# Attention followed by two MLPs: five of nine probability tiles of a head pair turned by TensorE in float32, with a float32 product with V

## The chip, the core and the metric

The kernel runs on one core of a Trainium2 chip. Five engines work side by side, each with an instruction queue of its own that is worked off in order: TensorE (PE) multiplies and transposes, VectorE (DVE) and ScalarE (ACT) do elementwise work and empty PSUM, GpSimd (POOL) does elementwise work between SBUF tiles, and SyncE (SP) issues transfers. The metric is device time in microseconds; lower is better.

## What is computed

```python
q_rot, k_rot = rotate(q), rotate(k)                  # 2 batches, 8 heads, 576 positions, width 64
scores = scale * q_rot @ k_rot.T
attn = exp(scores - max) ; attn /= attn.sum + 1e-9   # P, 576 x 576 for each head
x = (attn @ v)                                       # -> 1152 tokens x 512
h = x @ w_in ;  g = h * tanh(softplus(h)) ; x2 = g @ w_out      # 512 -> 2048 -> 512
h = x2 @ w_in2; g = h * sigmoid(1.702 h)  ; out = g @ w_out2
```

All of it is in float32 accuracy. The MLP weights come as 64-bit numbers and are narrowed on the core.

## The kernel before

**Two stretches.** Attention goes first, then the two MLPs, which are long dense runs of products on PE. Attention handles heads in pairs: 8 pairs, one after the other, overlapped by the order of the code.

**One pair.** Queries and keys are rotated (`rope_ops`), turned on PE (`turn`: 8 transposes for q, 8 for k, 3 instructions for the last 64 positions) and split by ACT and DVE into a high and a low part, tile `qk`. The 576 queries of two heads make nine tiles of 128 rows: tiles 0 to 7 are four chunks c of two heads each (tile n is head n % 2 of chunk n // 2), and tile 8 holds the last 64 queries of both heads. For each tile PE makes the scores (`s_mm`, 12 matmuls for the two heads of a chunk, 6 for tile 8) into a slot of two PSUM banks, `st`; DVE finds the row maximum (`s_max`, L260); ACT takes the exponential into the float32 tile `e` or `er` (`s_exp`, L275).

**Turning P.** The product with V needs P with keys on partitions. In most tiles P is split into a high and a low half-precision part: the high part by ACT or DVE (`p_split`, L288 or L290), the low part mostly by POOL (L294), into a tile `p`; a transposing transfer (`p_turn`, L339) writes it to `pt`. In pairs 0 to 6 tiles 7 and 8, and in the last pair tiles 4 to 8, go another way: PE transposes `e` in float32 (`e_turn`: one idle matmul and 5 transposes, `et`), and ACT or DVE write the high part to `pt` and DVE the low part (`e_part`).

**Product with V.** Group 0 holds chunks 0 and 1 (256 columns), group 1 holds chunks 2 and 3 and tile 8 (320 columns). `pv_mm` runs 5 blocks of keys by 3 terms (high by high, high by low, low by high) by 2 heads: 30 half-precision matmuls into the bank `pvps`, each head on its own 64 output columns of the array. The row sums, inverted and turned on PE (`r_mm`, `rps`), scale the result (`pv_end`), which becomes `x`.

**PSUM.** Three slots of two banks (`pss`, tag "s") take the score tiles and the turned tiles `et`; one bank (`bank`, tag "m") is shared by `tps` (turned q and k), `rps` and `vps`; one bank is `pvps`. A new tenant of a slot or of the shared bank waits until its last one has been read.

**Order.** `Plan` plays all attention operations through with written-down costs and ranks (`RANK`), chooses an engine where several are allowed, and writes the code in the order of the starts. Where it sees PE idle for more than 0.2 and `pvps` is not collecting a product, it puts idle matmuls (`keep_clock`, L641, 128x192, here called fillers). The MLP begins with products `h`, and pieces of the last pair's second product stand between them.

Of the kernel before, what the change touches and what calls it, by code (L numbers as in the profile page):

```python
# [22 lines left out]
def kernel(  # L23
# [62 lines left out]
    QK, vh, PT, sums, rrs, vs = ({} for _ in range(6))  # L86
# [13 lines left out]
    raw = [att.tile([128, 2, 2, (4, 4, 5)[i], 64], F32, name=f"raw{i}", bufs=1) for i in range(3)]  # L100
    P2 = [att.tile([128, 2, 2, KB * 128], F16, name=f"p2_{i}", bufs=1) for i in range(3)]
    x = xp.tile([128, 2, KD, TOK], F32R, tag="x", name="x")

    def heads(p):
        return p // NPAIR, 2 * (p % NPAIR)

    def load(ps, i):
# [3 lines left out]
        SP.dma_start(  # L111
            out=raw[i][:, j:j + len(ps), :, 0:4, :].rearrange("p j a t d -> p (j a) (t d)"),
            in_=src.rearrange("a (p t) d -> p a (t d)", t=4),
        )
# [6 lines left out]
    def load_v_rest(ps):  # L121
        src = v.rearrange("b h s d -> (b h) s d")[2 * ps[0]:2 * ps[-1] + 2, MAIN:S, :]
        SP.dma_start(
            out=raw[2][0:64, :, :, 4, :].rearrange("p j a d -> p (j a) d"), in_=src.rearrange("a s d -> s a d")
        )

    def v_max(ps):

        t = att.tile([128, 4], F32, tag="vs", name="vs", bufs=2)
        for j, p in enumerate(ps):  # L130
            vs[p] = t
            ACT.activation(
                out=junk, in_=raw[2][:, j].rearrange("p a t d -> p (a t d)"), func=AF.Abs, scale=1.0 / VEXP,
                accum_out=t[:, 2 + j:3 + j],
            )
# [12 lines left out]
    def v_high(p, eng):  # L148
        t = vh[p] = att.tile([128, 2, 2, KB, 64], F16, tag="vh", name="vh")
        if eng is ACT:  # L150
            ACT.activation(out=t[:, 0], in_=raw[2][:, p % 2], func=AF.Copy, scale=vs[p][:, 0:1])
        else:
            eng.tensor_scalar(t[:, 0], raw[2][:, p % 2], vs[p][:, 0:1], 1.0, op0=ALU.mult, op1=ALU.mult)

    def v_low(p):
        t = vh[p]
        DVE.scalar_tensor_tensor(  # L157
            out=t[:, 1], in0=raw[2][:, p % 2], scalar=vs[p][:, 0:1], in1=t[:, 0], op0=ALU.mult, op1=ALU.subtract
        )
# [147 lines left out]
    def pt_tile(p, g):  # L307
        if (p, g) not in PT:
            PT[p, g] = att.tile([128, 4 * KB, GW[g]], F16, tag=f"pt{g}", name=f"pt{g}")
# [4 lines left out]
    def e_turn(p, n):  # L314

        ps = pss.tile([128, 2, 512], F32, tag="s", name="et").rearrange("p b c -> p (b c)")[:, 0:KB * 128]
        e = ebuf[p, n // 2][:, n % 2]
        PE.matmul(out=ps[:, S - 64:KB * 128], lhsT=idle[:, 0:128], rhs=idle[:, 0:128], start=True, stop=True)
        for kb in range(KB):
            k = min(128, S - 128 * kb)  # L320
            PE.transpose(ps[0:k, 128 * kb:128 * kb + 128], e[:, 128 * kb:128 * kb + k], ident)
        return ps.rearrange("p (k q) -> p k q", q=128)

    def e_part(p, n, ps, eng, hl):
        c, h = n // 2, n % 2
        if n < 8:
            t = pt_tile(p, c // 2)[:, :, COL[c]:COL[c] + 128]
            ts = [t[:, KB * (2 * h + i):KB * (2 * h + i) + KB] for i in range(2)]
        else:
            t = pt_tile(p, 1)[:, :, 128:192].rearrange("k (h i b) q -> k h i b q", h=2, i=2)  # L330
            ts = [t[:, :, i] for i in range(2)]
            ps = ps.rearrange("k b (h q) -> k h b q", h=2)
        p_split(eng, hl, ts, ps)
# [310 lines left out]
    class Plan:  # L644
# [5 lines left out]
            raw0=1, raw1=1, raw2=1, rest=1, diag=1, rtmp0=3, rtmp1=2, m=1, pv=1, qk=2, s=3, nm=4, e=3,  # L650
            er=1, p2=3, pt0=2, pt1=2, sums=2, rc=2, rr=1, rrr=2, rb0=2, rb1=2, xf=2, vs=2, vh=2,
# [5 lines left out]
        WINDOW, BUSY = 10.24 / 3, 3400  # L657
        PORT = {"rope", "rest", "first rope", "first rest", "high", "low", "v low", "xh", "xl", "w", "rr", "rw"}
# [44 lines left out]
        def play(self):  # L703
# [10 lines left out]
            order, moved, work = [], 0.0, {}  # L714
# [23 lines left out]
            while True:  # L738
# [17 lines left out]
                if e == "PE":  # L756
# [10 lines left out]
                    done = product(start, o["cost"][e] + 0.1 * (o["rank"][1] != last), o["work"])  # L767
                    last = o["rank"][1]
                else:
                    done = start + o["cost"][e]  # L770
                free[e] = done
                if e == "POOL":
# [26 lines left out]
            self.work = work  # L799
# [8 lines left out]
        "rw": 6664.6, "rw DVE": 7052.1, "rw POOL": 5435.6, "first": 5746.8, "load q": 6506.8, "load k": 6297.4,  # L808
        "load rest": 5690.8, "load v": 5839.4, "load w": 7656.6, "rest": 7370.3, "rope": 6798.8, "turn": 4961.8,
        "v max": 5287.7, "v high": 6725.5, "v low": 5649.6, "s": 6645.6, "max": 4994.2, "exp": 5948,  # L810
        "high": 7357.5, "low": 5556, "pt": 7298.5, "rc": 4907.1, "rr": 6797.4, "rm": 7136.3, "rb": 6944.6,
        "pv": 7853.9, "xf": 7140.7, "xh": 6655.5, "xl": 5772.8, "w": 5847.2, "u": 6863.7, "first load q": 5110.4,
        "first load k": 5319.2, "first load rest": 5774.5, "first rope": 7126.2, "first rope POOL": 5698.3,
        "first turn": 5576.8, "first rest": 7569.6, "first rest DVE": 5260.8, "rest DVE": 6867.2,
        "rope POOL": 6505.7, "high DVE": 6486.6, "low DVE": 7209.9, "xh DVE": 7381.7, "xl DVE": 5695.4,
        "et": 5024.9, "eh": 4889.8, "el": 6845.6, "v high ACT": 7107, "w POOL": 5692.1, "rr ACT": 7178.7,
        "rr DVE": 6476.3, "eh DVE": 6583.4, "load sin": 6991.7, "load cos": 7296.4,
# [4 lines left out]
    PV_CUTS = (0, 5, 10, 15)  # L822
# [3 lines left out]
    turns_of = [SOME_TURNS] * (NP - 1) + [PE_TURNS]  # L826
    ET8 = 5
    uses = []
    for p in range(NP):
        late = [("et", p - 1, n) for n in turns_of[p - 1] if n < 8] if p else []  # L830
        for n in TILES[p]:
            uses.append(("s", p, n))
            if n == 3:
                uses += late
            if n == ET8:
                uses.append(("et", p, 8))
    uses += [("et", NP - 1, n) for n in PE_TURNS if n < 8]
# [29 lines left out]
    def plan_v(ps):  # L867
# [3 lines left out]
            needs=[("raw", p, 2), ("st", p, 1)] + [("qk", 0, 2)] * (p == 0), makes=("vm", p), holds=[("raw2", p // 2)] + hold)  # L871
# [9 lines left out]
    def plan_pair(p):  # L881
# [22 lines left out]
        last = p == NP - 1  # L904
        turns = turns_of[p]

        def first(n):
            d["s", n] = s_tile()
            s_mm(p, [(n, d["s", n], 0)])

        def second(n):
            parts = [(n, d["s", n], 1)]
            if n % 4 < 3:
                d["s", n + 1] = s_tile()
                parts.append((n + 1, d["s", n + 1], 0))
            s_mm(p, parts)

# [11 lines left out]
        for at, n in enumerate(TILES[p]):  # L929
            g, c = base + at, n // 2  # L930
            s_at = ring["s", p, n]
            e, p2 = (("e", 4 * p + c), ("p2", 4 * p + c)) if n < 8 else (("er", p), None)
# [11 lines left out]
            if n in turns:  # L944
                gr = min(c // 2, 1)
                hold = [ring["et", p, n], (f"pt{gr}", p + 2 * gr)]
                add("PE", 0.6, (g, "et"), lambda n=n: d.update({("et", n): e_turn(p, n)}), work=640,
                    needs=[("en", p, n)], makes=("et", p, n), holds=hold + [e])
                add(None, dict(ACT=0.684, DVE=0.73), (g, "eh"), lambda eng, n=n: e_part(p, n, d["et", n], eng, 0),
                    needs=[("et", p, n)], makes=("eh", p, n), holds=hold)  # L950
                add("DVE", 0.735, (g, "el"), lambda n=n: e_part(p, n, d["et", n], DVE, 1), needs=[("eh", p, n)],
                    makes=[("el", p, n), ("pt", p, gr)], holds=hold)
                continue
            hs = tuple(h for h in range(2) if 2 * c + h not in turns)
            hss = [hs] * (n == 2 * c + hs[-1])
            gr = c // 2
            for hs in hss:
                w = len(hs)
                for h in hs:
                    n1 = 2 * c + h  # L960
                    add(None, dict(ACT=0.573, DVE=0.37), (g + n1 - n, "high"),
                        lambda eng, c=c, h=h: p_high(p, c, (h,), eng), needs=[("en", p, n1)],
                        makes=("hi", p, c, h), holds=[e, p2])
# [202 lines left out]
```

## Time and profile before

| | |
|---|---|
| three timed runs | 562.92, 564.01, 564.64 us (median 564.01) |
| profiled execution | span 560.9 us from the first to the last instruction; the page lists no device time of its own for it |
| first MLP product on PE | starts at 156.19 us |
| PE, DVE, ACT, POOL busy, whole span | 97%, 64%, 49%, 20% |
| PE busy of that in fillers (L641) | 29.6 us, 275 matmuls, all before 156.19 us |
| granted TensorE clock | 1.00 in every stretch looked at |

The page tells shares over the whole span, and these mix the two stretches. The MLP (from 156.19 us) has PE busy nearly throughout, so a time there is set by PE. In the attention stretch several engines are busy most of the time, so one has to ask stretch by stretch which is full and who waits for whom. A row of the stretches view lists for each engine its busy time and, in brackets, the number of its instructions. Two cautions: a duration contains the time in which the result drains, which overlaps the next instruction, so the cost of a run of matmuls is read as the distance from its start to the start of the next; and a few per cent of the matmul records can be missing.

### The profile page before, as it was taken

The numbers are of one execution on the slowest core, as the hardware profiler recorded it, in microseconds if no ns is written. First come the engines' busy times: TensorE is split into PE (matmuls) and PEld (weight loads), VectorE is DVE, ScalarE is ACT, GpSimd is POOL, SyncE is SP. The second block draws the span as 40 slices with busy tenths as digits, with TensorE's granted clock in tenths as the row PEclk, the third lists the DMA queues.
The fourth block names the chain that finished last, engine by engine and source line by source line (L and its number), as shares of the span: only waits on it lengthen the run. The fifth ranks groups of instructions, "written<-read, shape, count | busy, mean of one in ns | idle before, by whom it ended". The sixth has DMA issues, their size and how long they took to land.

```text
span 560.9 us, 9318 instructions
## 1 busy us (share of the span) xinstructions
PE 543.1 (97%) x3669; PEld 496.3 (88%) x3669; DVE 357.1 (64%) x692; ACT 273.1 (49%) x591; POOL 114.6 (20%) x101
## 2 busy tenths in 40 slices
PE   8989799899999999999999999999999999999997
PEld 7867577677789999999999999999988889998885
DVE  7999989999957867255887557856620337821030
ACT  2988799688827651222666213265510325751000
POOL 4888798757500000000000000000000000000000
PEclk9999999999999999999999999999999999999999
DMA  6899899888913434133343322423220125200032
GB/s 165 155 227 156 190 184 169 169 152 178 168 61 114 146 102 131 61 99 128 126 148 106 120 76 43 130 91 113 77 76 0 37 77 148 77 1 0 1 112 57
DMA packets 107787, 61.29 MB, mean 109 GB/s; under 512 B 73568, under 2 KB 104544, under 8 KB 107744
## 3 DMA queue, kind: packets, MB, share of 16 engines
q1 hardware_dynamic: 107456, 60.37, 43.8%
q8 instruction: 29, 0.48, 0.4%
q10 hardware_dynamic: 288, 0.33, 0.2%
q14 instruction: 14, 0.11, 0.1%
HBM read 40.96 MB, written 2.36 MB: 77 GB/s over the span
## 4 chain that ended last, share of the span: by engine, by line
PE 78%; DVE 12%; ACT 5%; issue 3%; DMA 1%; SPq 1%; POOL 0%; DVEq 0%; ACTq 0%; POOLq 0%
PE h L532 31%; PE acc L599 16%; PE acc L613 16%; PE pvps L532 4%; DVE spill L260 4%; ACT e L275 3%; PE pvps L599 2%; PE st L249 2%; PE pvps L613 2%; PE pvps L369 2%; DVE p L290 1%; DVE qk L236 1%; DVE vh L157 1%; PE pvps L641 1%; PE tps L220 1%
## 5 line engine op out<-in xcount | busy, mean ns | idle before, releaser
L532 PE MATMUL h<-x,whl 128*128 128x384 f32 x1008 | 178.6, 335 | 0.0
L532 PEld LDWEIGHTS h<-x,whl 128*128 128x128 f32 x1008 | 174.8, 188 | 1.0 <-issue 1.0
L463 DVE TENSOR_TENSOR whl<-wf,whl 128x512 fp32r<-128x512 f32 x63 | 43.6, 692 | 95.1 <-ACT whl L462 95.1
L613 PE MATMUL acc<-whl,g 128*128 128x512 f32 x384 | 88.9, 389 | 0.0
L599 PE MATMUL acc<-g,whl 128*128 128x384 f32 x504 | 88.6, 334 | 0.0
L599 PEld LDWEIGHTS acc<-g,whl 128*128 128x128 f32 x504 | 87.5, 188 | 0.0
L613 PEld LDWEIGHTS acc<-whl,g 128*128 128x128 f32 x384 | 72.0, 188 | 14.9
L294 POOL TENSOR_TENSOR p<-e,p 128x576 f16<-128x576 f32 x52 | 71.7, 1395 | 18.8 <-DVE p L290 10.5
L569 DVE TENSOR_TENSOR g<-t,g 128x384 fp32r<-128x384 f32 x96 | 53.1, 554 | 30.1 <-ACT g L579 30.1
L462 ACT ACTIVATE whl<-wf 128x512 fp32r<-128x512 f32 x64 | 40.1, 627 | 59.4 <-DVE wf L481 40.1
L578 ACT ACTIVATE t<-h 128x384 f32<-128x384 f32 x84 | 40.6, 483 | 40.6 <-PE h L532 40.4
L260 DVE CUSTOM_DVE_ANT_1 spill<-st,shift 128x576 f16<-128x576 f32 x72 | 54.1, 752 | 5.5 <-PE st L249 1.2
L275 ACT ACTIVATE e<-st,nm 128x576 f32<-128x576 f32 x64 | 47.2, 742 | 10.7 <-DVE nm L260 9.2
L579 ACT ACTIVATE g<-t 128x384 fp32r<-128x384 f32 x96 | 50.6, 527 | 3.1
L249 PE MATMUL st<-qk 64*128 64x288 f32 (+1 forms) x432 | 45.6, 311 | 4.6 <-ACT e L275 3.1
L249 PEld LDWEIGHTS st<-qk 64*128 64x128 f32 (+1 forms) x432 | 34.9, 185 | 13.4 <-ACT e L275 6.9
L478 DVE SCALAR_TENSOR_TENSOR wf<-wraw,wf 128x512 int32<-128x512 int32 x64 | 44.2, 691 | 1.6
L481 DVE SCALAR_TENSOR_TENSOR wf<-wraw,wf 128x512 int32<-128x512 int32 x64 | 44.1, 689 | 1.4
L369 PE MATMUL pvps<-pt,vh 128*64 128x256 f16 (+1 forms) x480 | 36.8, 290 | 0.1
L641 PE MATMUL pvps<-idle 128*128 128x192 f16 x275 | 29.6, 260 | 1.7 <-DVE shift L1021 1.0
L369 PEld LDWEIGHTS <-vh 128*64 128x64 f16 x480 | 23.5, 109 | 8.3 <-issue 5.7
L1107 DVE TENSOR_TENSOR acc<-acc,acc 128x512 f32<-128x512 f32 x8 | 5.5, 688 | 37.1 <-PE acc L613 37.1
(101 smaller groups left out, 528.9 us busy)
## 6 DMA issues: line engine op xcount, KB each, us to landing
wraw<-in_moe_w_in_dram SPq DMA_DIRECT2D x32, 512.0 KB, 3.7
wraw<-in_moe_w_out_dram SPq DMA_DIRECT2D x32, 512.0 KB, 3.5
raw<-in_v_dram SPq DMA_DIRECT2D x4, 512.0 KB, 4.7
raw<-in_q_dram SPq DMA_DIRECT2D x3, 512.0 KB, 4.3
raw<-in_k_dram SPq DMA_DIRECT2D x3, 512.0 KB, 5.2
out_dram<-acc SPq DMA_DIRECT2D x10, 128.0 KB, 2.4
out_dram<-acc SPq DMA_DIRECT2D x4, 256.0 KB, 2.4
raw<-in_q_dram SPq DMA_DIRECT2D x2, 256.0 KB, 4.0
```

Source lines behind the costliest of these rows:

```text
L249: PE.matmul(out=st[:, g, 0:HALF], lhsT=t[r, ql, c0:c0 + 128], rhs=t[r, kl, KC + HALF * g:KC + HALF * g + HALF], start=(i == 0), stop=(i == 2),
L260: DVE.tensor_tensor_reduce(out=spill, in0=st[:, :, 0:HALF], in1=shift[:, 0:1].unsqueeze(2).to_broadcast([128, 2, HALF]), scale=-SCALE, sca ...
L275: ACT.activation(out=ebuf[p, n // 2][:, n % 2, :].rearrange("p (g s) -> p g s", g=2), in_=st[:, :, 0:HALF], func=AF.Exp, bias=nm, scale=SC ...
L294: eng.tensor_tensor(out=t[1], in0=src, in1=t[0], op=ALU.subtract)
L369: PE.matmul(out=ps[64 * a:64 * a + 64, 0:W], lhsT=w[:, vl, a, kb, :], rhs=pt[:, KB * (2 * a + pl) + kb, :], start=(n == 0), stop=(n == len ...
L478: lambda: DVE.scalar_tensor_tensor(out=t, in0=hi, scalar=-0x40000000, in1=t, op0=ALU.bitwise_and, op1=ALU.bitwise_or),
L481: lambda: DVE.scalar_tensor_tensor(out=t, in0=lo, scalar=29, in1=t, op0=ALU.logical_shift_right, op1=ALU.bitwise_or),
L532: PE.matmul(out=ps[:, 0:UN], lhsT=w[:, wl, 128 * kk:128 * kk + 128], rhs=src[:, xl, kk, cols(u)], start=(kk == 0 and (wl, xl) == X_LAST[0] ...
L569: DVE.tensor_tensor(out=gl, in0=t, in1=f32(gh), op=ALU.subtract)
L579: ACT.activation(out=gh, in_=t, func=AF.Copy)
L599: PE.matmul(out=ps[:, 0:UN], lhsT=w[:, wl, 128 * f:128 * f + 128], rhs=g[:, gl, 4 * half + f, cols(u)], start=(half == 0 and f == 0 and (w ...
L613: PE.matmul(out=ps, lhsT=g[:, gl, f, 128 * t:128 * t + 128], rhs=w[:, wl, :], start=(f == 0 and (gl, wl) == TERMS[0]), stop=(f == FC - 1 a ...
```

## The change

- Tiles 4 to 8 of every pair go through PE now; only chunks 0 and 1 are split and sent through a transposing transfer.
- Turned tiles stay float32 and are not split. `e_turn` turns the first 512 keys of both heads of a chunk into one PSUM slot (8 transposes); tile 8 goes through the shared bank (4 transposes, `eps`). `e_out` copies them out, one copy for each head, on ACT or DVE.
- The last 64 keys of tiles 4 to 8 are turned in one step in the shared bank (`rest_turn`: 4 transposes and 2 float32 matmuls) and copied once (`rest_out`, tile `pr`).
- The product of group 1 is in float32 straight from V (`raw_v`): 5 blocks by 2 heads. V has two buffers, and a third transfer puts the last positions of the odd head on partitions 64 to 127 too. Tile `p` has two buffers in place of three.
- New ranks, a new sequence of PSUM slots (`SLOTS`), and other rules where the planner charges a change of shape on PE.

```diff
-            parts[p, c] = P2[(4 * p + c) % 3]
+            parts[p, c] = P2[(2 * p + c) % 2]
...
+    def turn_keys(ps, e):
+        for kb in range(4):
+            PE.transpose(ps[:, 128 * kb:128 * kb + 128], e[:, 128 * kb:128 * kb + 128], ident)
+
+    def e_turn(p, c):
+        if c == 4:
+            ps = bank("eps")
+            turn_keys(ps, ebuf[p, 4][:, 0])
+            return ps
+        ps = s_tile()
+        for h in range(2):
+            turn_keys(ps[:, h], ebuf[p, c][:, h])
+        return ps
+
+    def e_out(p, c, ps, h, eng):
+        t = pt_tile(p, 1)
+        if c < 4:
+            copy(eng, t[:, h, :, COL[c]:COL[c] + 128], ps[:, h].rearrange("k (b q) -> k b q", b=4))
         else:
+            copy(eng, t[:, :, :, 128:192], ps.rearrange("k (b h q) -> k h b q", b=4, h=2))
+
+    def rest_turn(p):
+        ps = bank("eps")
+        for c in (2, 3):
+            b = slice(COL[c], COL[c] + 128)
+            PE.transpose(ps[:, b], ebuf[p, c][:, 1, S - 128:S], ident)
+            PE.transpose(ps[0:64, b], ebuf[p, c][:, 0, MAIN:S], ident)
+        e = ebuf[p, 4][:, 0]
+        PE.matmul(out=ps[:, 128:192], lhsT=e[:, S - 128:S], rhs=ident[:, 64:128], start=True, stop=True)
+        PE.matmul(out=ps[0:64, 128:192], lhsT=e[:, MAIN:S], rhs=ident[:, 0:64], start=True, stop=True)
+        return ps[:, 0:GW[1]]
...
+        if g:
+            for kb in range(n0, n1):
+                for a in range(2):
+                    r = slice(64 * a, 64 * a + 64)
+                    k, src = (r, PR[p][r]) if kb == KB - 1 else (slice(0, 128), pt[:, a, kb, :])
+                    PE.matmul(
+                        out=ps[r, 0:W], lhsT=v_of(p)[k, p % 2, a, kb, :], rhs=src, start=(kb == 0), stop=(kb == KB - 1),
+                    )
+            return
...
-        "rw": 6664.6, "rw DVE": 7052.1, "rw POOL": 5435.6, "first": 5746.8, "load q": 6506.8, "load k": 6297.4,
+        "first": 6035.8, "load sin": 5486.1, "load cos": 8298.2, "first load rest": 4721.1, "first rest DVE": 5553.6,
...
-    PE_TURNS = (4, 5, 6, 7, 8)
-    SOME_TURNS = (7, 8)
+    TURNS = (2, 3, 4)
+    SLOTS = ("s0 s1 s2 s3 e3- s8 s4 s5 s6 s7 e2", "s8 s0 s1 e3- s2 s3 s4 s5 s6 s7 e2", "e3-")
```

The order in which the instructions stand moves too. On PE before, where the product of the first pair's group 1 begins behind a turned tile 8 and turned row sums (`vh` is split V):

```order
L318 LDWEIGHTS idle
L318 MATMUL et<-idle 128x128
L321 MATMUL et<-ident,er 128x128 x4
L321 MATMUL et<-ident,er 64x128
L385 MATMUL rps<-ident,rr 128x128 x2
L369 LDWEIGHTS vh
L369 MATMUL pvps<-pt_417,vh 64x320
```

The same work in the middle of the attention stretch after (`pr` and `raw_v` are the turned last keys and V, both float32):

```order
L400 MATMUL pvps<-pt_767,raw_v_89 64x320 x2
L256 MATMUL st<-qk 128x288 x12
L400 MATMUL pvps<-pt_767,raw_v_89 64x320 x2
L353 MATMUL eps<-ident,e 128x128
L354 MATMUL eps<-ident,e 64x128
L353 MATMUL eps<-ident,e 128x128
L354 MATMUL eps<-ident,e 64x128
L356 MATMUL eps<-ident,er 128x64
L357 MATMUL eps<-ident,er 64x64
L400 MATMUL pvps<-pt_767,raw_v_89 64x320 x2
L256 MATMUL st<-qk 128x288 x12
```

The product of group 1 is now cut into single blocks of keys with scores and turned keys between them. On PE ahead of that place, after, three tenants of the shared bank (`rps`, `eps`, `tps`) follow one another:

```order
L424 MATMUL rps<-ident,rr 128x128 x2
L256 MATMUL st<-qk 128x288 x12
L327 MATMUL eps<-ident,er 128x128 x4
L327 MATMUL st<-ident,e 128x128 x8
L227 MATMUL tps<-ident,rtmp_667 128x128
```

One run of scores or one turned chunk stands between two tenants. On DVE, in a late pair before, a copy of a half of a turned tile stands with casts and low parts of P:

```order
L290 CAST p_1_91<-e 128x576
L294 TENSOR_TENSOR p_1_91<-e,p_1_91 128x576
L294 TENSOR_TENSOR pt_1890<-et,pt_1890 128x2x5x64
L260 ISA spill,nm<-st,shift 128x576
L260 ISA nm 128x1
```

After, DVE takes both heads of a turned chunk one after the other, and a half of the turned q or k stands behind them:

```order
L267 ISA spill,nm<-st,shift 128x576
L267 ISA nm 128x1
L297 COPY pt_1765<-st 128x4x128 x2
L243 TENSOR_TENSOR qk<-tps,qk 128x512
L378 RECIPROCAL rc<-rc 128x5
```

Before the first MLP product, the order of before holds 275 fillers, spread over the attention stretch, and that of after 147, the last of them ahead of the sixth run of scores.

## Rows read from the trace of the kernel before

**Rows 1.** The stretches view: head, rest of attention, MLP.

```profile
0.00:30.40 30.40, 28.47 (x270) 25.05 (x271) 25.48 (x58) 18.82 (x43) 19.77 (x24) 1.00 0.74 162
30.40:156.19 125.79, 113.80 (x1212) 89.44 (x1211) 118.35 (x255) 104.79 (x258) 94.84 (x78) 1.00 0.92 177
156.19:560.90 404.71, 400.84 (x2192) 381.86 (x2190) 213.30 (x381) 149.47 (x290) 0.00 (x0) 1.00 0.27 84
```

**Rows 2.** The waits of PE in attention: total us, times, longest.

```profile
PE st L249 <- ACT e L275: 3.1, 5, 1.1
PE tps L220 <- DVE qk L236: 2.1, 2, 1.9
PE rps L385 <- DVE qk L236: 1.7, 1, 1.7
```

**Rows 3.** The timeline of PE, four places: start, us, instruction, count.

```profile
62.38 1.09 PE L220 MATMUL tps<-ident,rtmp 128*128 128x128 f32 x8
...
67.92 1.06 PE L220 MATMUL tps<-ident,rtmp 128*128 128x128 f32 x8 [1.86 <-DVE qk L236]
...
77.70 0.98 PE L641 MATMUL pvps<-idle 128*128 128x192 f16 x10 [0.45 <-DVE xf L401]
78.62 1.05 PE L249 MATMUL st<-qk 64*128 64x288 f32 x12
79.60 0.87 PE L369 MATMUL pvps<-pt,vh 128*64 128x320 f16 x10
80.40 1.09 PE L220 MATMUL tps<-ident,rtmp 128*128 128x128 f32 x8
81.43 0.87 PE L369 MATMUL pvps<-pt,vh 128*64 128x320 f16 x10
...
86.91 0.22 PE L318 MATMUL et<-idle 128*128 128x128 f16 x1
...
87.61 0.74 PE L369 MATMUL pvps<-pt,vh 128*64 128x256 f16 x10
...
145.17 2.23 PE L369 MATMUL pvps<-pt,vh 128*64 128x320 f16 x30
147.33 1.40 PE L249 MATMUL st<-qk 64*128 64x288 f32 x12
```

**Rows 4.** Groups of PE instructions in attention, by shape: count, busy us, mean ns.

```profile
L369 PE MATMUL pvps<-pt,vh 128*64 128x320 f16 x210 | 17.7, 303 | 0.0
L369 PE MATMUL pvps<-pt,vh 128*64 128x256 f16 x240 | 16.5, 276 | 0.1
L321 PE MATMUL et<-ident,e 128*128 128x128 f32 x44 | 6.7, 274 | 0.0
L387 PE MATMUL rps<-rrr,block 128*128 128x64 f32 x16 | 2.7, 248 | 0.0
```

**Rows 5.** Groups of DVE, ACT and POOL in attention, by shape.

```profile
L290 DVE CAST p<-e 128x576 f16<-128x576 f32 x20 | 13.8, 699 | 0.2
L294 DVE TENSOR_TENSOR pt<-et,pt 128x640 f16<-128x640 f32 x19 | 15.4, 819 | 0.3
L178 DVE TENSOR_TENSOR rtmp<-raw,rsin 128x512 f32<-128x512 f32 x9 | 9.5, 1051 | 2.2 <-DMA raw<-in_q_dram 1.8 <-DMA raw<-in_k_dram 0.4
L236 DVE TENSOR_TENSOR qk<-tps,qk 128x512 fp32r<-128x512 f32 x16 | 10.8, 677 | 0.9 <-ACT qk L233 0.5
L288 ACT ACTIVATE p<-e 128x576 f16<-128x576 f32 x33 | 21.8, 682 | 0.1
L294 POOL TENSOR_TENSOR p<-e,p 128x576 f16<-128x576 f32 x52 | 71.7, 1395 | 18.8 <-DVE p L290 10.5 <-ACT p L288 4.4 <-issue 2.8
```

**Rows 6.** The timeline of DVE: the same cast at two places.

```profile
16.57 0.81 DVE L290 CAST p<-e 128x576 f16<-128x576 f32 x2
...
89.21 1.53 DVE L290 CAST p<-e 128x576 f16<-128x576 f32 x1
```

**Rows 7.** The timeline of SP: four transposing transfers in a row.

```profile
84.01 15.41 SPq L339 DMA_TRANSPOSE pt<-p  x4
```

More of the change, by code (lines that the diff above doesn't have):

```diff
@@ L85 @@
     GW = [256, 320]
-    QK, vh, PT, sums, rrs, vs = ({} for _ in range(6))
+    QK, vh, PT, PR, sums, rrs, vs = ({} for _ in range(7))
     ident = const.tile([128, 128], F32, name="ident")
@@ L308, in pt_tile @@
         if (p, g) not in PT:
-            PT[p, g] = att.tile([128, 4 * KB, GW[g]], F16, tag=f"pt{g}", name=f"pt{g}")
+            if g:
+                PT[p, g] = att.tile([128, 2, 4, GW[1]], F32, tag="pt1", name="pt1")
+                PR[p] = att.tile([128, GW[1]], F32, tag="pr", name="pr")
+            else:
+                PT[p, g] = att.tile([128, 4 * KB, GW[0]], F16, tag="pt0", name="pt0")
         return PT[p, g]
     COL = (0, 128, 0, 192)
[L314 to L322, printed above, removed]
@@ L335, in p_turn, with rest_out @@
+    def rest_out(p, ps, eng):
+        pt_tile(p, 1)
+        copy(eng, PR[p], ps)
     def p_turn(p, c, hs):
@@ L766, in play @@
                         order.append((first, len(order), lambda n=n: keep_clock(n)))
-                    done = product(start, o["cost"][e] + 0.1 * (o["rank"][1] != last), o["work"])
-                    last = o["rank"][1]
+                    shape = self.SHAPE.get(o["rank"][1], 0)
+                    done = product(start, o["cost"][e] + 0.095 * (shape != last), o["work"])
+                    last = shape
                 else:
@@ L954, in plan_pair @@
[L954 to L963, printed above, removed]
[L964 to L968 removed]
+            if c in TURNS:
+                if n in (4, 6):
+                    continue
+                hold = [ring["et", p, c] if c < 4 else ("m", ("e", p))]
+                add("PE", 0.89 if c < 4 else 0.45, (g, "et"), lambda c=c: d.update({("et", c): e_turn(p, c)}),
+                    work=1024 if c < 4 else 512, needs=[("e", p, c)], makes=("et", p, c), holds=hold + [e])
+                for h in range(2 if c < 4 else 1):
+                    add(None, dict(ACT=0.5, DVE=0.62), (g, "eh"), lambda eng, c=c, h=h: e_out(p, c, d["et", c], h, eng),
+                        needs=[("et", p, c)], makes=("pt", p, 1), holds=hold + [("pt1", p)])
+                if n == 7:
+                    hold = [("m", ("er", p))]
+                    add("PE", 0.69, (g, "er"), lambda: d.update({"er": rest_turn(p)}), work=640,
+                        needs=[("e", p, c) for c in TURNS], makes=("er", p),
+                        holds=hold + [("e", 4 * p + 2), ("e", 4 * p + 3), ("er", p)])
+                    add(None, dict(ACT=0.36, DVE=0.42), (g, "er"), lambda eng: rest_out(p, d["er"], eng),
+                        needs=[("er", p)], makes=("pr", p), holds=hold + [("pt1", p)])
+                continue
@@ new lines, in plan_pair @@
+            add(None, dict(ACT=0.573, DVE=0.37), (g, "high"), lambda eng, c=c, h=n % 2: p_high(p, c, (h,), eng),
+                needs=[("en", p, n)], makes=("hi", p, n), holds=[e, p2])
+            add(None, dict(POOL=1.24, DVE=0.64), (g, "low"), lambda eng, c=c, h=n % 2: p_part(p, c, (h,), eng, 1),
+                needs=[("hi", p, n)], makes=("lo", p, c), holds=[e, p2])
+            if n % 2:
+                add("SP", 0.35 + 1.12 * 2, (g, "pt"), lambda c=c: p_turn(p, c, (0, 1)), needs=[("lo", p, c)],
+                    makes=("pt", p, 0), holds=[p2, ("pt0", p)], move=2.1 * 2, lead=TURN)
@@ L1052 @@
     add("PE", 0.0, (END, "s"), swap, makes="swap",
-        needs=[("e", NP - 1, c) for c in range(5)] + [("el", NP - 1, n) for n in PE_TURNS])
+        needs=[("e", NP - 1, c) for c in range(5)] + [("pt", NP - 1, 1)])
     for i in range(4):
```

142 lines of the change are left out of this document (56 added, 86 removed), and 3 rows, old and new, of the table RANK.

## Prediction

> **What bounds the kernel now.** I first split the span at the first MLP product, 156.2 us, in the stretches view [rows 1]. Behind it PE is busy for 400.8 of 404.7 us, 99%: the MLP is set by PE, and the change doesn't touch its work. So only the time at which the MLP starts can move, and a little work that stands among its first products. Ahead of it, between 30.4 and 156.2 us, DVE is busy for 118.35 of 125.8 us, 94.1%. PE has 113.8 (90%), and part of that is fillers, which do nothing for the result; ACT has 104.8 (83%), POOL 94.8 (75%). DVE is what is full. The waits of PE say the same from the other side: its longest are for the readers of PSUM, 3.1 us for the exponential of ACT and 2.1 + 1.7 us for DVE's half of a turned q or k [rows 2]. PE itself has room: 142.3 us busy up to 156.2, less 275 fillers. Ten fillers take 0.92 us (77.70 to 78.62) [rows 3].
>
> So the question is what happens if work moves from DVE, ACT, POOL and the transfers to PE, and whether PE's fillers are enough room for it.
>
> **PE, step by step**, up to the first MLP product, by distances from start to start.
>
> Turned tiles. One of the 19 of before takes 0.70 us with its idle matmul (86.91 to 87.61) [rows 3]: 13.3 us go. Eight transposes take 1.03 (80.40 to 81.43) [rows 3], and the new chunk is eight: 16 x 1.03 = 16.5. Tile 8 is half of that: 8 x 0.51 = 4.1. The step for the last keys is four transposes, 0.51, and two float32 matmuls of 64 columns. Such matmuls are in the trace (L387): 8 in the order, 16 records, so each is carried out as two, with 248 ns a record that mostly overlap [rows 4]. I take 0.4 for the two, 0.9 a step, 7.2 in all. New 27.8, old 13.3: +14.5 us.
>
> The product of group 1. Old: three runs of ten a pair, 0.80 us each (79.60 to 80.40) [rows 3]; seven pairs lie ahead of the MLP, 16.8 us. The new one, float32 on 64 columns of the array, is nowhere in the trace. Bounds: 64 columns more cost 27 ns in half precision (303 against 276), so one pass of 320 columns is 0.135 us. A float32 transpose of 128 columns takes 274 ns, where half precision by that slope would take 222: two passes. A record of L387 with 64 columns takes 248 against 195: three passes [rows 4]. With two records a matmul is 4 to 6 passes, 0.54 to 0.81 us. Whether both heads run side by side decides more: in half precision they do (0.16 us for two matmuls where one after the other would be 0.27). Low end 35 x 0.54 = 18.9 us; one after the other 70 x 0.54 = 37.8; high end 70 x 0.81 = 56.7. I take the low end, since the same two halves of the array already run side by side, plus 1.5 for the cuts: 20.4, so +3.6 us.
>
> Cuts: thirty matmuls in one run take 2.16 us (145.17 to 147.33), in three runs 2.40 [rows 3], so each of the four changes of array shape costs 0.06. In the order such changes go from 137 to 149; that is 0.7 of the 1.5. The Trainium skill, TensorEngine Tiling, Key Properties, says that a change of tiling mode drains TensorE. By that rule cutting the product into single blocks speaks against the change; the row shows the drain to be cheap.
>
> Fillers: 275 become 147, 128 x 0.092 = -11.8 us.
>
> PE busy ahead of the MLP: 142.3 + 14.5 + 3.6 - 11.8 = 148.6 us. PE takes over more than its fillers gave.
>
> **DVE, ACT, POOL, transfers** [rows 5]. DVE loses 9 casts (0.70 each, -6.3), 26 halves of turned tiles (0.82, -21.3), 3 rotations (1.05, -3.2). It gains 28 copies of 512 float32 out of PSUM, nearest row 0.68 (+19.0), 5 of 320, some 0.5 (+2.5), and 5 low parts, 0.70 (+3.5). That is -5.8. A cast takes 0.40 alone and 1.53 beside POOL [rows 6]; POOL drops from 52 low parts to 26 (-36 us of 1.4 each), so DVE's other work shortens too: 0 to 5 us, I take 3. DVE falls from 143.8 to about 135. ACT loses 12 high parts at 0.68, about -8 of 123.6; its 12 copies replace as many turned halves.
>
> Transfers: a transposing transfer of two tiles takes 3.85 us of the SP queue (15.41 for four) [rows 7]; a pair had three and a half, now two. The loads behind them on SP start earlier, and the extra load of V's last positions is small. I cost this and the second V buffer at nothing: no wait for a transfer is among PE's long ones [rows 2]. Tile `p` with two buffers is taken again only one pair later, some 17 us, against 3.85; if that cover were gone, a high part would wait on ACT or DVE with maxima and exponentials queued behind it. The float32 product no longer needs split V in group 1; split V stays for group 0, so nothing is saved.
>
> Head: in the new order four turned blocks stand ahead of the first scores, not two; against it, fillers leave there. Between -1 and +2 us; I take 0.
>
> **The sum.** If DVE stayed the bound at its 94.1%, the rest of attention would take (135 - 25.5) / 0.941 = 116.4 us and the MLP would start at 146.8. PE needs 148.6 - 28.5 = 120.1 us in the same stretch, so PE becomes the bound. How full can an engine be that waits for others in order? DVE, as the bound, reached 94.1%; PE in the MLP reaches 99%. 94.1%: start at 158.0. 99%: 151.7. I take the middle, 97%: 30.4 + 123.8 = 154.2, so -2.0 us. Behind the first MLP product the last pair's product costs 2.7 plus 0.4 for five cuts against 2.4: +0.7. Together -1.3 us: span 559.6 for the profiled 560.9. The three timed runs have a median of 564.0, 3.1 above the span; the same step gives **562.7 us**, with 560.2 to 566.5 for 99% and 94.1%. A measurement of this kernel tells about 0.3%, 1.7 us: same means 562.3 to 565.7.
>
> **Rivals.**
>
> *Cheaper PE work.* A run of eight new transposes needs no second operand added, and 0.90 is possible; with 0.7 for the last keys and no cost of cuts PE's work is 5.7 us less, and at 97% the MLP starts at 148.3: **556.8**. For it: the 1.03 us is read from transposes that add up two operands, and the new ones have one. Against: the count of instructions is the same, and so are the changes of shape.
>
> *The shared bank takes over as the wait.* It gets two more tenants in every pair, `eps` twice, and the order puts a single run of scores or one turned chunk, about 1 us of PE, between tenants, in which ACT or DVE has to be free to copy the old one out. PE waited 3.8 us for that bank's reader [rows 2], once for 1.86 us, when a turned block of 62.38 was still there at 67.92 [rows 3]. Behind a waiting transpose everything on PE is held up, the scores among it, and DVE and ACT then starve. With 0.5 us at each of the 16 new tenants that is +8.0: **570.7, slower**. It decides from 0.2 us a tenant (565.9). Against it: DVE has 9 us more room, and the two halves of P that queued there are gone.
>
> *Heads one after the other.* If float32 matmuls don't overlap on the halves of the array: +17.4 ahead of the MLP and 2.5 behind: **582.6, slower**.
>
> *The clock falls.* Fillers vanish from the later pairs, and more of PE's work is transposes. In all three stretches the granted clock was 1.00, that is 2.4 GHz, with 10% idle and nineteen turned tiles in between [rows 1]. A tenth of PE's 120.1 us at 1.2 GHz would add 12.0: **574.7**. The Trainium skill, TensorE: Matmul & The Clock Gate, Part 4, says that transposes don't count as PE work the way matmuls do and don't bring the clock up. By that rule the new chunks would endanger the clock; this trace has no stretch in which it fell.
>
> **Chances.** The forecast with its band 0.55 (0.25 faster, 0.24 same, 0.06 slower), cheaper PE work 0.16, the shared bank 0.16 (0.13 slower), one after the other 0.09, the clock 0.04. Faster 0.41, same 0.27, slower 0.32. The range 555.5 to 571.5 holds the first three cases nearly whole; about 0.17 is left out.
>
> **What would show it.** PE between 30 and 150 us should be busy for 96 to 98% with hardly a filler, DVE below 90%; the MLP should start at 152 to 157 us. A run of two float32 matmuls should take about 0.55 us; 1.1 means one after the other. If waits of PE for the readers of `eps`, `tps` and `rps` add up to more than 7 us, the shared bank it is. A granted clock below 1.00 would show the fourth rival. The forecast is wrong in its core if PE is below 92% there without these waits: then a chain from DVE or ACT sets the pace, and my choice of 97% fails.

## The result and the profile after

The changed kernel takes **557.52 us** (median of four executions, 557.29 to 558.24) against 563.96 for the kernel before on the same chip: ratio 0.9889, 95% interval 0.9875 to 0.9904, so 6.4 us (1.1%) faster. The forecast was 562.7 with a range of 555.5 to 571.5: right sign, time in the range, but 5.2 us too high. The profiled execution spans 556.5 us for 560.9 before. Of the executions below, one of `a_dve` (605.14 us at a mean granted clock of 0.852) is left out of the ratio.

The stretches view after, cut at 30.2 us and at the first MLP product (stretch, length, busy time and count of PE, PEld, DVE, ACT, POOL, granted clock, DMA share, GB/s); it answers to [rows 1]:

```profile
0.00:30.20 30.20, 27.59 (x253) 24.55 (x253) 23.11 (x57) 18.28 (x43) 15.37 (x23) 1.00 0.65 168
30.20:149.93 119.73, 118.44 (x1139) 89.64 (x1138) 107.92 (x257) 98.72 (x246) 68.23 (x61) 1.00 0.62 128
149.93:556.50 406.57, 402.42 (x2182) 381.44 (x2180) 211.58 (x378) 149.59 (x291) 0.00 (x0) 1.00 0.28 84
```

The MLP starts at 149.93 us, 6.26 earlier. In the middle stretch PE is busy for 118.44 of 119.73 us (98.9%), DVE for 90.1%, where [rows 1] has 90% and 94.1%. The MLP stretch is 1.86 us longer than before, so 4.4 us are left of the 6.26 in the span.

The waits of PE ahead of the MLP (us in all, times, longest), which answer to [rows 2]; the first and the third lie in the head:

```profile
PE pvps L233 <- DVE diag L207: 1.3, 1, 1.3
PE rps L424 <- DVE qk L243: 1.0, 1, 1.0
PE pvps L680 <- DVE shift L1045: 1.0, 1, 1.0
PE tps L233 <- DVE qk L243: 0.2, 1, 0.2
PE tps L227 <- DVE qk L243: 0.2, 1, 0.2
```

Three waits for a reader of the shared bank are left, 1.4 us together, for 3.8 in [rows 2]; no wait for a slot of scores is named any more. The eight waits of [rows 2] came to 6.9.

The costliest changed groups ahead of the MLP, by shape (count, busy us, mean ns, idle before), which answer to [rows 4, 5]:

```profile
L400 PE MATMUL pvps<-pt,raw_v 128*64 128x320 f32 x112 | 18.5, 445 | 0.0
L400 PE MATMUL pvps<-pr,raw_v 64*64 64x320 f32 x28 | 5.3, 454 | 0.0
L327 PE MATMUL st<-ident,e 128*128 128x128 f32 x128 | 16.8, 275 | 0.0
L680 PE MATMUL pvps<-idle 128*128 128x192 f16 x147 | 16.8, 274 | 1.0 <-DVE shift L1045 1.0
L297 DVE COPY pt<-st 128x512 f32<-128x512 f32 x24 | 15.6, 684 | 0.9 <-ACT pt L295 0.9
L297 DVE CAST p<-e 128x576 f16<-128x576 f32 x11 | 6.3, 571 | 0.2 <-issue 0.2
L185 DVE TENSOR_TENSOR rtmp<-raw,rsin 128x512 f32<-128x512 f32 x6 | 4.0, 686 | 1.9 <-DMA raw<-in_q_dram 1.9
L301 POOL TENSOR_TENSOR p<-e,p 128x576 f16<-128x576 f32 x26 | 34.3, 1332 | 14.6 <-DVE p L297 10.5 <-issue 2.8 <-POOL rtmp L189 1.0
```

A copy of a turned half costs DVE 684 ns, where one of the two passes over a turned tile cost 819. The cast and the rotation, unchanged instructions, fall from 699 to 571 and from 1051 to 686 ns while POOL's low parts go from 52 to 26. The traces show why for the casts. Where POOL was idle as a cast began, it took 430 to 461 ns. Where POOL was in an elementwise instruction (five of 20 casts before, three of 11 after), the cast ended 0.31 to 0.32 us after that instruction did, and took up to 1.54 us.

The timeline of PE at two places (start, us, instruction, count), which answers to [rows 3]:

```profile
48.18 0.33 PE L353 MATMUL eps<-ident,e 128*128 128x128 f32 x1
...
49.20 0.76 PE L400 MATMUL pvps<-pr,raw_v 64*64 64x320 f32 x4
49.88 1.06 PE L256 MATMUL st<-qk 64*128 64x288 f32 x12
...
51.32 1.04 PE L327 MATMUL st<-ident,e 128*128 128x128 f32 x8
52.20 1.04 PE L227 MATMUL tps<-ident,rtmp 128*128 128x128 f32 x8
...
86.66 2.37 PE L400 MATMUL pvps<-pt,raw_v 128*64 128x320 f32 x16
88.96 0.43 PE L146 MATMUL vps<-ident,vs 128*128 128x128 f32 x2
```

A turned chunk: 51.32 to 52.20, 0.88 us. The step for the last keys: 48.18 to 49.20, 1.02. Four blocks of the float32 product in a row: 86.66 to 88.96, 2.30 us, 0.575 a block of two heads; a block alone: 0.68 (49.20 to 49.88). The two heads run side by side: in that run the records start in pairs, one of each head within 7 ns, and a pair starts about 0.27 us behind the last one (0.32 the first time).

**PE's account.** I added up the whole timeline of PE up to the first MLP product, from start to start, less the idle times it names:

| us of PE | before | after | change | forecast |
|---|---|---|---|---|
| old turned tiles | 12.8 | 0 | -12.8 | -13.3 |
| turned chunks, 16 | 0 | 14.5 | +14.5 | +16.5 |
| tile 8 and last keys, 8 each | 0 | 11.4 | +11.4 | +11.3 |
| products with V | 32.3 | 37.6 | +5.3 | +3.6 |
| scores | 43.0 | 40.4 | -2.6 | 0 |
| fillers | 27.7 | 15.9 | -11.8 | -11.8 |
| rest | 27.1 | 26.3 | -0.8 | 0 |
| **work** | **142.9** | **146.2** | **+3.3** | **+6.3** |
| **named waits** | **12.2** | **2.7** | **-9.5** | **-8.3** |

PE does more work than before and starts the MLP earlier, because its waits are gone. The forecast of the waits is 156.2 - 142.3 = 13.9 before and 154.2 - 148.6 = 5.6 after; both hold some 1.0 us ahead of PE's first instruction, which the measured row doesn't.

### The profile page after: what moved, and what is told of

Same layout as the page of the kernel before. It is cut to its first block, busy times and chain, and to the rows that moved or that the text cites. A ratio compares the mean times of both kernels' runs of the same rounds, so it can differ in the third digit from the quotient of the medians.

```text
span 556.5 us, 9033 instructions
## 1 busy us (share of the span) xinstructions
PE 548.4 (99%) x3571; PEld 495.6 (89%) x3571; DVE 342.6 (62%) x691; ACT 266.6 (48%) x578; POOL 83.6 (15%) x83
## 4 chain that ended last, share of the span: by engine, by line
PE 95%; DVE 3%; DMA 1%; issue 1%; SPq 0%; DVEq 0%
PE h L571 32%; PE acc L638 16%; PE acc L652 16%; PE st L256 7%; PE pvps L400 5%; PE pvps L571 4%; PE st L327 2%; PE pvps L408 2%; PE pvps L638 2%; PE tps L227 2%; PE pvps L652 2%; DVE spill L267 1%; PE rps L424 1%; PE pvps L680 1%; DMA rest<-in_k_dram 1%; PE eps L327 1%
## 5 line engine op out<-in xcount | busy, mean ns | idle before, releaser
L256 PE MATMUL st<-qk 64*128 64x288 f32 (+1 forms) x432 | 42.7, 309 | 0.0
L301 POOL TENSOR_TENSOR p<-e,p 128x576 f16<-128x576 f32 x26 | 34.3, 1332 | 14.6 <-DVE p L297 10.5
L571 PE MATMUL pvps<-x,whl 128*128 128x384 f32 x144 | 27.2, 334 | 0.0
L514 DVE TENSOR_SCALAR wf<-wraw 128x512 int32<-128x512 int32 x64 | 26.9, 420 | 0.0
L571 PEld LDWEIGHTS pvps<-x,whl 128*128 128x128 f32 x144 | 25.2, 188 | 0.0
```

The costliest lines, as they stand in the source:

```text
L256: PE.matmul(out=st[:, g, 0:HALF], lhsT=t[r, ql, c0:c0 + 128], rhs=t[r, kl, KC + HALF * g:KC + HALF * g + HALF], start=(i == 0), stop=(i == 2),
L571: PE.matmul(out=ps[:, 0:UN], lhsT=w[:, wl, 128 * kk:128 * kk + 128], rhs=src[:, xl, kk, cols(u)], start=(kk == 0 and (wl, xl) == X_LAST[0] ...
```

## Experiments

The theory from the two traces: **before, DVE set the pace and PE had room; after, PE is full.** The rivals: the new order alone brought the gain; or turning more tiles on PE did, whatever the form. Changes below are against the runs of the kernel before that were made beside them (563.63 to 563.77 us) or against the 557.52 of the changed kernel; its own runs of before had 563.96, so differences of some 0.3 us between the groups mean nothing.

### What held the kernel before

`b_pe` turns tile 8's first four key blocks twice: 32 more transposes on PE.

```diff
-        for kb in range(KB):
+        for kb in [0, 1, 2, 3] * (n == 8) + list(range(KB)):
```

> The kernel before with four of the transposes of tile 8 made twice in each pair (the second time the same result), 32 in all, some 0.12 us each, 3.8 us on PE. Theory 1 (PE has room before): 0 to +1.2 us, 564 to 565. Rival (PE's queue sets the pace already): +3 to +4 us, 567 to 568.

Measured: 563.71 us, ratio 1.0005 (0.9990 to 1.0019), +0.1. Where the mean granted clock was 0.998 or more, the spans are 561.5 to 561.8 us in six executions, for 560.7 to 561.3 in twelve of before. So 0.1 to 0.8 us of the extra PE work shows.

`b_dve` adds one DVE instruction to each pair, into a tile that nobody reads, behind the fifth maximum:

```diff
...
+        calls[0] += 1
+        if calls[0] % 9 == 5:
+            DVE.tensor_tensor(out=extra, in0=ident[:, 0:1].to_broadcast([128, 512]), in1=ident[:, 1:2].to_broadcast([128, 512]), op=ALU.add)
```

> The kernel before with one more elementwise instruction on DVE in each head pair (128x512, out of a constant into a tile that nobody reads), 8 in all, some 0.69 us each, 5.5 us together; order and planner unchanged. Theory 1 (before, DVE sets the pace of attention at 94% busy): nearly all of it shows, +4 to +5.5 us, 568 to 569.5. Rival (PE's queue with the PSUM slots sets the pace already before, DVE's load is only high): at most +1.5 us, 564 to 565.5.

Measured: 570.71 us, ratio 1.0129 (1.0112 to 1.0146), +7.1. The group of the added instructions in the trace of `b_dve`:

```profile
L269 DVE TENSOR_TENSOR extra<-ident 128x512 f16<-128x512 f32 x8 | 8.7, 1093 | 0.0
```

Of 8.7 us added, 82% shows. Part of that is the clock, in two neighbouring stretches of `b_dve`:

```profile
60.00:65.00 5.00, 2.26 (x19) 1.54 (x17) 4.86 (x9) 2.77 (x9) 3.04 (x2) 0.88 0.99 210
65.00:70.00 5.00, 5.00 (x33) 3.54 (x31) 3.08 (x7) 3.21 (x8) 4.49 (x4) 0.50 0.43 83
```

PE waited for more than half of the first, and the granted clock was 0.50, that is 1.2 GHz, in the whole of the second. All four executions of `b_dve` have a mean clock of 0.991 to 0.994 and span 568.8 to 569.0 us; the five of before with 0.992 to 0.994 span 562.9 to 564.5. Against those, 4.3 to 6.1 us are left, still far above the rival's 1.5.

`b_half` goes the other way: the maximum is taken over 288 of 576 keys.

```diff
-            out=spill, in0=st[:, :, 0:HALF], in1=shift[:, 0:1].unsqueeze(2).to_broadcast([128, 2, HALF]), scale=-SCALE,
+            out=spill[:, 0], in0=st[:, 0, 0:HALF], in1=shift[:, 0:1].to_broadcast([128, HALF]), scale=-SCALE,
```

> The kernel before with the maximum over the first 288 keys, the same relief of some 22 us for DVE. If DVE set the pace there, and PE had only its own 114.0 us to do in the stretch, the MLP starts at 30.2 + 114.0 / 0.989 = 145.5 us at best, 10.7 earlier; half of that if ACT and POOL come next. Theory 'DVE bound before': 5 to 11 us less than before. Rival (PE, fillers counted, or the transfers set the pace before): under 2 us.

Measured: 555.87 us, ratio 0.9868 (0.9847 to 0.9889), -7.9. The middle stretch of `b_half`:

```profile
30.20:148.95 118.75, 111.18 (x1208) 88.37 (x1205) 103.37 (x253) 103.02 (x258) 94.78 (x77) 1.00 0.99 186
```

Relieving DVE of 21.6 us (72 maxima, 752 to 452 ns) brings 7.9 us, more than the 6.4 of the whole change, and the MLP starts at 148.95. So DVE did set the pace before. What holds `b_half` isn't settled: PE is busy for 93.6%, DVE and ACT for 87%; the DMA share has gone from 0.92 to 0.99.

### What holds the changed kernel

`a_pe` doubles tile 8's four transposes in the changed kernel:

```diff
             turn_keys(ps, ebuf[p, 4][:, 0])
+            turn_keys(ps, ebuf[p, 4][:, 0])
```

> The changed kernel with the four transposes of tile 8 made twice in each pair, 32 in all, some 0.12 us each, 3.8 us on PE. Theory 1 (PE is full after): all of it shows, +3.4 to +4.2 us, 561 to 561.8. Rival (a chain through DVE or ACT sets the pace): below +1.5 us, under 559.

Measured: 560.56 us, ratio 0.9950 (0.9932 to 0.9967), +3.0 on the changed kernel. By the same account of its trace, tile 8 and the last keys take 15.0 us for 11.4. So 3.0 of 3.6 us show, a little less than expected, where 0.1 to 0.8 did before.

`a_dve` makes the edit of `b_dve` in the changed kernel.

> The changed kernel with the same 8 instructions on DVE, 5.5 us. Theory 1 (PE sets the pace now; DVE is 90% busy between 30 and 150 us and has 11.8 us free there): at most +1.5 us, 557.5 to 559. Rival (DVE still sets the pace, the gain is only its smaller load): +4 to +5.5 us, 561.5 to 563.

Measured: 562.99 us, ratio 0.9991 (0.9974 to 1.0007), +5.5 on the changed kernel. Its middle stretch, and the two longest waits of PE behind the head:

```profile
30.20:154.59 124.39, 119.42 (x1142) 89.85 (x1139) 114.55 (x264) 99.79 (x248) 69.96 (x61) 1.00 0.60 123
```

```profile
PE rps L430 <- DVE qk L244: 3.0, 4, 1.4
PE vps L147 <- DVE qk L244: 0.8, 1, 0.8
```

Here the first form of the theory fell. It read the 11.8 us that DVE isn't busy in the stretch as room. 63% of the 8.7 us shows, and the way is plain: the turned q or k in the shared bank waits for DVE's half, and on PE the next tenant, `rps` or `vps`, with all that is queued behind it, waits too. By the same account of its trace, PE's work up to the MLP is 146.3 us, as much as after (146.2), and its named waits are 7.3 for 2.7.

`a_dve2` puts the same instructions behind the first maximum of a pair (`% 9 == 1`), to tell the load from an unlucky place.

> The changed kernel with the same eight extra DVE instructions of 1.09 us, 8.7 us in all, put behind the first maximum of each pair in place of the fifth. There they cost 5.5 us. Theory 'level' (DVE's load counts wherever it stands): 4 to 7 us more than the changed kernel. Rival 'place' (the fifth maximum was an unlucky spot, DVE has 11.8 us free): at most 1.5.

Measured: 561.54 us, ratio 0.9960 (0.9941 to 0.9978), +4.0: 51% of the 7.9 us that the eight take there; the six executions lie between 559.61 and 562.43. The place decides between 4.0 and 5.5; most is load.

`a_less` takes PE work away: key blocks 1 and 2 of the float32 product are left out, and the output isn't the reference's.

```diff
-            for kb in range(n0, n1):
+            for kb in (k for k in range(n0, n1) if k not in (1, 2)):
```

> The changed kernel without blocks 1 and 2 of the five key blocks in the float32 product of group 1, in all pairs: 14 blocks of about 0.57 us ahead of the MLP and 2 pieces of 0.69 behind are left out, and the order of the rest is the same. Theory 1 (PE is full, DVE comes next): PE's 118.4 us fall to about 110.4, DVE has 107.9; the MLP starts 5 to 8 us earlier, and with the two pieces behind it the time falls by 6.4 to 9.6, to 548 to 551. Rival (another chain sets the pace): only the pieces behind show, 556.

Measured: 554.06 us, ratio 0.9833 (0.9817 to 0.9850), -3.5 on the changed kernel, between what the two expected. Its middle stretch:

```profile
30.20:147.82 117.62, 112.52 (x1081) 86.49 (x1077) 106.62 (x256) 98.15 (x244) 67.92 (x61) 1.00 0.61 129
```

PE's busy time in the stretch falls by 5.9 us, but the MLP starts only 2.1 earlier (the rest comes from the work behind its start). PE is down at 95.7%; DVE stays at 90.6%. That suggests a second theory: **PE is full, and DVE's chain stands just behind it.** Then a lighter DVE alone must bring little, and both cuts together more than their sum.

`a_half` is the changed kernel with the edit of `b_half`.

> The changed kernel with the row maximum taken over the first 288 of the 576 keys (the other half is left out; a maximum of a part serves as well to shift the exponential). 72 DVE instructions of 0.75 us shrink to an estimated 0.45, some 22 us of DVE's 131 ahead of the MLP. Theory 'level' (PE is full and DVE stands just behind it): PE waits for 1.3 us only in the 119.7 us stretch, so the gain is 0 to 1.5 us. Rival 'DVE sets the pace' (PE only looks full, its instructions stretched): 5 us or more.

`a_half_less` has both cuts.

> The changed kernel with both cuts: the maximum over half of the keys, and key blocks 1 and 2 of the float32 product left out. The second cut alone took 5.9 us of PE out of the stretch but moved the first MLP product by only 2.1. Theory 'level': DVE's chain stopped it, so with DVE light the MLP starts at about 30.2 + 112.5 / 0.989 = 144.0 us, 5.9 earlier than in the changed kernel, and the total gains 7 to 8 us on it. Rival 'order alone' (the places of the instructions, not DVE's load, held it back): the same as with the second cut alone, 3.5 us.

| | us | ratio (interval) | against the changed kernel | MLP starts at |
|---|---|---|---|---|
| `a_half` | 555.87 | 0.9859 (0.9845 to 0.9874) | -1.65 | 147.49 |
| `a_less` | 554.06 | 0.9833 (0.9817 to 0.9850) | -3.5 | 147.82 |
| `a_half_less` | 549.91 | 0.9755 (0.9740 to 0.9769) | -7.6 | 143.58 |

The middle stretch of `a_half`, then that of `a_half_less`:

```profile
30.20:147.49 117.29, 117.13 (x1128) 88.67 (x1126) 93.48 (x255) 96.79 (x244) 67.66 (x60) 1.00 0.64 129
```

```profile
30.20:143.58 113.38, 111.02 (x1071) 85.40 (x1070) 93.62 (x254) 96.38 (x244) 67.74 (x60) 1.00 0.66 134
```

In `a_half` DVE is down to 79.7%, and PE, busy for all but 0.2 us, lets the time go down by only 1.65, a little over the 1.5 that I had set as the end. With DVE light, the smaller product brings 555.87 - 549.91 = 6.0 us; with DVE as it is, 3.5. The MLP starts at 143.58, close to the 144.0 that a full PE was expected to give, with PE busy for 97.9% of the stretch. So the second theory holds: two bounds nearly level, and "90% busy" was nearly full for DVE. `a_half` and `b_half` take the same 555.87 us: once DVE is relieved otherwise, the change brings nothing more.

### The parts of the change

`b_rank` is the kernel before with the new ranks where both kernels have the same kind of operation.

> The kernel before with the planner's ranks of the changed kernel, for every kind of operation that both have; the work is the same, the order is another. Theory 1 (the gain is work taken off DVE): no gain, 562.5 or slower. Rival (the gain is the new order): at least half of the gain, 560.8 or less.

Measured: 569.29 us, ratio 1.0105 (1.0090 to 1.0120), +5.7. New ranks alone are no gain, against the rival on the order. (The new ranks without the new operations aren't the new order, so the price isn't theirs in the changed kernel.)

`b_five` turns tiles 4 to 8 on PE in all pairs, but still splits them and multiplies in half precision; the sequence of slots is adapted.

```diff
-    turns_of = [SOME_TURNS] * (NP - 1) + [PE_TURNS]
+    turns_of = [PE_TURNS] * NP
...
```

> The kernel before with tiles 4 to 8 of every pair turned by PE, as in the change, but still split in a high and a low half-precision part and with the half-precision product. 21 more turned tiles: DVE gets some 21 low parts and a share of the high parts of 0.82 us, +17 to +22 us, and loses perhaps 8 us of casts; POOL loses 21 low parts, SP 21 tiles of transfers. Theory 1 (DVE sets the pace, the float32 product is what lets the split go): slower by 5 to 14 us, 569 to 578. Rival (the gain is the fewer transposing transfers and POOL's smaller load, which slows DVE): 562 or faster.

Measured: 583.87 us, ratio 1.0370 (1.0349 to 1.0391), +20.2, beyond the 5 to 14 expected. The passes of DVE over turned tiles in `b_five`:

```profile
L294 DVE TENSOR_TENSOR pt<-et,pt 128x640 f16<-128x640 f32 x40 | 32.3, 817 | 2.9 <-ACT pt L288 2.9
L290 DVE CAST pt<-et 128x640 f16<-128x640 f32 x8 | 6.6, 821 | 0.1
```

Those are 38.9 us of DVE. In the changed kernel its copies of turned tiles take 20.7: 15.6 for the 24 shown above, 2.7 for four of tile 8 and 2.4 for five of the last keys. Turning more tiles without dropping the split loads the engine that is full. How much of the 20 us comes from my sequence of slots is open: neither DVE (88%) nor PE (89%) is full in that trace, and all four executions have a mean granted clock of 0.991, so part of it is clock. What fewer transposing transfers bring by themselves wasn't tested; the DMA share of the middle stretch fell from 0.92 to 0.62, but no named wait of PE ahead of the MLP is for a transfer in either trace.

`a_cutlast` joins the pieces of the last pair's product behind the MLP's start: three in place of five.

```diff
-            cuts = PV_CUTS[gr]
+            cuts = (0, 2, 4, 5) if gr and p == NP - 1 else PV_CUTS[gr]
```

> The changed kernel with the last pair's float32 product, which stands among the first MLP products, cut in three pieces (blocks 0 and 1, 2 and 3, 4) in place of five; the rest in the same order. Theory (each cut costs a change of array shape twice and a restart of the MLP's weights): 0.4 to 0.9 us faster, 556.7 to 557.1. Rival (cuts are free, the pieces fill waits there): within 0.2 us of 557.5.

Measured: 556.67 us, ratio 0.9881 (0.9866 to 0.9896), -0.85 on the changed kernel (0.5 where each is taken against its own runs of before); its MLP stretch:

```profile
149.26:555.00 405.74, 401.60 (x2182) 381.61 (x2180) 212.05 (x378) 149.81 (x291) 0.00 (x0) 1.00 0.27 84
```

It is 0.83 shorter than after, about 0.4 for each of two breaks. This computes what the reference asks and beats both kernels. `a_half` also does on these inputs, but a maximum of half of the keys no longer bounds the exponent, so other inputs could overflow. Both edits together weren't run.

## Why the prediction was right in sign and 5.2 us too high

The forecast's steps from the profile after: MLP start 154.2, measured 149.93 (-4.3); work behind it +0.7, measured +1.86 (+1.15); step from span to median 3.1, measured 557.52 - 556.5 = 1.0 (-2.1). Together -5.2. The sign was no great hit: -1.3 us lay within what the prediction called the same.

**DVE bounds before, PE after.** Right; `b_pe`, `b_dve` and `b_half` show the first, `a_pe` and `a_half` the second.

**PE's work, +6.3.** Measured +3.3. The fillers fit to 0.1, the last keys and tile 8 too. Mis-sized were the turned chunk (1.03 us; measured 0.91 on the mean) and the product (+5.3 for +3.6: single blocks take 0.69, not 0.58). The 1.03 was put down to the two operands of the transposes in [rows 3]. The rows show another reason, what stands behind them. Two places, the first before, the second after:

```profile
121.47 1.06 PE L220 MATMUL tps<-ident,rtmp 128*128 128x128 f32 x8
122.37 0.25 PE L641 MATMUL pvps<-idle 128*128 128x192 f16 x1
...
141.72 1.09 PE L327 MATMUL st<-ident,e 128*128 128x128 f32 x8
142.75 2.37 PE L400 MATMUL pvps<-pt,raw_v 128*64 128x320 f32 x16
```

Before, the eight with two operands take 0.85 to 0.90 us in the six places where work on the same shape of the array follows, and 1.00 to 1.03 in the ten where another shape follows. After, the new chunks with one operand take 0.87 to 0.94 in fourteen places of the first kind and 0.97 and 1.03 in the two of the second.

I also missed the scores: before, ten of 29 runs of twelve matmuls took 1.07 to 1.53 us and the others about 1.0; after, four of 25 took 1.10 to 1.17. The likely reason, only argued, is that inside a run the second head's slot was waited for without a wait being named.

**PE at 97%.** The forecast took the middle of 94.1% and 99%, with no reason for the middle; measured 98.9%. Of the 4.3 us by which the MLP starts too early for the forecast, 2.4 are PE's work (148.6 forecast, 146.2) and 1.9 are this step (5.6 us of waits forecast, 149.9 - 146.2 = 3.7 measured, the 1.0 before PE's first instruction included). The upper bound was the right one; that the other engines feed PE's queue well ahead there, as in the MLP, is the likely reason, but only argued.

**DVE falls to 135.** Measured 23.11 + 107.92 = 131.0. The relief from POOL's absence was taken at 3 us; the instructions that stayed ran 7.0 us shorter. Eleven casts are shorter by 128 ns each, six rotations by 365, and eight passes that split V (1304 to 878) by 426. That POOL is the reason is shown for the casts, and for the other two likely. So of the 12.8 us by which DVE's load falls, more than half is the same instructions running shorter, and the smaller part is instructions that are gone. I wrote that DVE "has 9 us more room"; as room it was worth little (`a_dve`). It was to fall below 90% in the middle stretch; it stands at 90.1%.

**Behind the MLP's start, +0.7.** The timeline after, five pieces of 0.69 us (152.22 to 152.91 is one) between runs of `h`:

```profile
152.22 0.76 PE L400 MATMUL pvps<-pt,raw_v 128*64 128x320 f32 x4
152.91 2.38 PE L571 MATMUL h<-x,whl 128*128 128x384 f32 x12
155.22 0.76 PE L400 MATMUL pvps<-pt,raw_v 128*64 128x320 f32 x4
155.91 1.86 PE L571 MATMUL h<-x,whl 128*128 128x384 f32 x9
157.70 0.76 PE L400 MATMUL pvps<-pt,raw_v 128*64 128x320 f32 x4
```

The pieces take 3.45 us against 3 x 0.80, +1.05. Of the other 0.8, half is in the runs of `h` that the two further pieces break: nine matmuls take 1.79 us (155.91 to 157.70), 0.199 each, where a run of 39 of before took 0.176 each (6.87 in all, from 164.93 to 171.80), so 0.2 a run. The other 0.4 I didn't place. `a_cutlast` gives 0.4 us for a break, product and run together; the forecast took 0.08 (0.4 for five), from the slope within the product alone, and left out the run that is broken.

**From span to median, 3.1.** Of the 35 executions of the kernel before made beside the experiments, 12 have a mean granted clock of 0.998 to 1.000 and span 560.7 to 561.3 us; 23 have 0.992 to 0.997 and span 561.5 to 564.5. The profile that I predicted from was one of the 12. The device time is 1.9 above the span, and the median has another 1.1 or so of clock. The four executions after all have 0.998 to 1.000, and the time is 1.7 above the span; the profiled one (556.5) is the longest of the four, whose median is 555.8. So the 2.1 us are 1.1 of clock, 0.2 of what lies around the span, and 0.7 because the profile of after is on the long side. About 1 us of the gain of 6.4 is that the clock no longer falls; I had carried that loss over to the new kernel.

**The rivals.** *Shared bank*: the named waits are 1.4 us, below the 7 that would have shown it; but `a_dve` shows that this is the wait that comes next. *One after the other*: 0.575 us a block, not 1.1 (its +17.4 counts the 1.5 for the cuts on one side only; with it on both sides it is 18.9). *Clock*: 1.00 in all stretches. The Trainium skill, TensorE: Matmul & The Clock Gate, Part 4, would have put the clock in danger with more transposes; the trace doesn't show it, and it was the kernel with fewer transposes and more waits on PE that lost clock. *Cheaper PE work*, 556.8, came nearest in time, in part by luck: the chunks were cheaper, but not for the reason it gave, and the last keys (0.92 for 0.7) and the cuts were not. On the cuts, the Trainium skill, TensorEngine Tiling, Key Properties, says that a change of tiling mode drains TensorE; the trace agrees in that a block alone takes 0.69 us and 0.575 in a run of four.

## What to carry to other kernels

When work moves off the engine that sets the pace, add up the new engine's whole queue in order, useless work included (here it filled to the level that the same engine shows elsewhere in the trace); then look for the second engine, since a busy share of 90% can be nearly full when its instructions release what the first one waits for. Look also for instructions that stay and only get shorter: they were more than half of DVE's relief here. To learn whether an idle share is room, lengthen that engine's queue a little; to find a second bound, relieve both engines together and compare with the sum. Before adding a constant step from a profiled span to a median, look whether the profiled execution was a typical one.

## What the runs showed of the hardware that I had not expected

- The float32 product on two halves of the array: a matmul of 320 columns is two records of 445 to 454 ns, and two matmuls, one on each half, take 0.575 us in a run.
- The clock after a wait of PE. In `b_pe`, whose profiled execution has a mean granted clock of 0.990 and spans 565.9 us (the others 561.5 to 562.7), two neighbouring stretches read:

```profile
65.00:70.00 5.00, 3.13 (x36) 2.23 (x35) 5.00 (x6) 2.47 (x7) 2.83 (x2) 0.96 0.50 125
70.00:75.00 5.00, 5.00 (x41) 4.14 (x42) 3.59 (x11) 4.52 (x12) 3.21 (x3) 0.69 0.83 195
```

PE was idle for 1.9 of 5 us, with DVE busy throughout; in the next five the mean granted clock was 0.69, a mixture of 2.4 and 1.2 GHz. One wait is paid twice there, as in `b_dve`. That the kernel before lost its 1 us in the same way is likely, but the trace that I have of it is of an execution without a fall.

- DVE's sum of two broadcast float32 columns, 512 elements, took 984 to 1093 ns; a copy of 512 float32 elements took 684.
